# Moving the weights 16 bytes against the moving data in an FFT and feed-forward kernel

## The chip, the cores and the metric

The kernel runs on one core of one Trainium2 chip. The metric is the device time of one execution in microseconds; lower is better. The shown time of the kernel before is a median of three runs.

## The reference, cut to what matters

The reference takes the real part of a two-dimensional Fourier transform of `x` and puts every row of it through a feed-forward layer with a piecewise activation. All data are float32.

```python
batch, seq, dim = 8, 3008, 256          # x; d_ff = 2048
X = np.fft.fft(np.fft.fft(x, axis=1), axis=2).real.astype(np.float32)
h = X.reshape(-1, 256) @ w_in           # [24064, 2048]
g = np.where(h >= 1, h, np.where(h <= -1, 0.0, (h + 1) ** 2 / 4))
return (g @ w_out).astype(np.float32)   # [24064, 256]
```

The weights arrive as float64.

## The kernel before, in words

The eight batches are worked off one after the other. The transform of a batch is split into a first stage (`stage1`, seven or eight pieces), one small Nyquist product and a second stage (`stage2`, six pieces). The pieces of batch b + 1 are strewn between the matmuls of batch b. The last step of a second-stage piece is `stage2_split`: ScalarE copies the PSUM result to `pqh` (the high part, float32r) and VectorE writes the rest to `pql` (the low part, float32r).

The feed-forward part works in units. A unit is one batch, one of three chunks `k` of transform columns, and one of 16 slices `f` of d_ff; there are 8 x 3 x 16 = 384 units. Chunk 0 has 482 columns, chunks 1 and 2 have 512 (`WIDTH`). Products are made nearly float32-exact by three float32r matmuls in place of one: high weight by high data, low weight by high data, high weight by low data.

- `gemm1` (its matmuls stand on line L596) makes two PSUM tiles `uv` of a unit from three matmuls each: stationary `wh` or `wl`, moving `pqh` or `pql`. These are 6 matmuls per unit, 128 weights wide, 482 or 512 columns long.
- VectorE and ScalarE turn `uv` into the activation; `activate` and `low_halves` leave its high part in `gh` (ScalarE, L630) and its low part in `gl` (GpSimd, L647).
- `gemm2` (L684) adds the activation's product with `w_out` into four PSUM tiles `acc`: stationary `woh` or `wol`, moving `gh` or `gl`, 12 matmuls per unit. In the first 20 units, before `woh` and `wol` are made, it runs 4 native float32 matmuls on `g` and `wo` instead (`NATIVE`).

A matmul of this kernel is always two instructions on TensorE: the load of its 128 x 128 weights (PEld in the profile) and the streaming of the moving data (PE). The order of all work is written out by hand (`START`, `STEPS`, `AHEAD`, `AMID`) for the first 34 units; later it follows from the loop over units.

Where the operands lie in a partition of SBUF is set by tile sizes. `wh` and `wl` are four tiles of 8192 bytes, `woh` and `wol` tiles of 16384 bytes that take the place of raw weights loaded earlier (`raw_woh`, `raw_wol`), `pqh`, `pql`, `gh` and `gl` tiles of 4096 bytes, one row of 512 columns for each of two signs. All of these begin at multiples of 256 bytes, and a weight slice of a unit is a multiple of 512 bytes further on. `ZPAD` (40 floats ahead of the transform's `z`) and the width of `biases` (48 floats) keep what follows at such multiples. Chunk 0 alone is shifted: its 482 columns begin 28 floats, 112 bytes, into each row of its tiles (`SHIFT`). Since 28 + 512 columns would not fit in the row, the second split of chunk 0 writes only its 226 useful columns, in two parts.

Of the kernel before, what the change touches and what calls it, by code (L numbers as in the profile page):

```python
# [9 lines left out]
F32 = mybir.dt.float32  # L10
F32R = mybir.dt.float32r
U32 = mybir.dt.uint32
# [9 lines left out]
NB, S, D, FF = 8, 3008, 256, 2048  # L22
NA, NBB, NC = 64, 47, 24
P = 128
# [5 lines left out]
CH = 512  # L30
NCHUNK = 3
NFT = FF // P
ZPAD = 40
LAG = 4
SKIP = (7, 11)
EVICT_AHEAD = 150

C_ORDER = [*range(1, 8), 0, *range(8, NC)]
WIDTH = [7 * NA + 34, CH, CH]
SHIFT = [28, 0, 0]  # L40

G_ORDER = np.arange(P).reshape(XC, GPC, 2, 2).transpose(0, 3, 1, 2).reshape(-1)

# [76 lines left out]
RAW = {0: "gh", 1: "gh", 2: "woh", 3: "woh", 4: "woh", 5: "woh", 6: "wol", 7: "wol", 8: "wol", 9: "wol", 10: "rx", 11: "rx", 12: "rx", 13: "xt", 14: "pqh", 15: "pql"}  # L120
WORK = {1: "a", 2: "gl", 3: "a", 4: "h", 5: "a", 7: "a", 8: "h", 9: "gl", 11: "gl", 12: "gl", 13: "gl", 15: "gl", 14: "a"}
BUFS = {"h": 4, "a": 3, "gl": 4, "cv": 0, "rx": 3, "xt": 4}
# [3 lines left out]
LOW = {}  # L126
# [14 lines left out]
def fft_ffn_kernel(ctx: ExitStack, tc: tile.TileContext, x, xn, cst, w_in, w_out, out):  # L141
    nc = tc.nc

    wts = ctx.enter_context(tc.tile_pool(name="wts", bufs=1))
    sb = ctx.enter_context(tc.tile_pool(name="sb", bufs=1))
# [3 lines left out]
    xt, yt, zt, nyb, pq = {}, {}, {}, {}, {}  # L149
# [59 lines left out]
    cm = sb.tile([P, _OFF[6] - _OFF[2]], F32, tag="nyb", name="cm", bufs=4)  # L209
    mats = [[cm[:, (2 * m + h) * P : (2 * m + h + 1) * P] for h in range(2)] for m in range(2)]  # L210

    wh = [wts.tile([P, FF], F32R, name=f"wh{i}") for i in range(2)]
    wl = [wts.tile([P, FF], F32R, name=f"wl{i}") for i in range(2)]
    delta = wts.tile([P, NFT], F32, name="delta")
    biases = wts.tile([P, 48], F32, name="biases")
    for i, v in enumerate((0.5, -896.0 * 128, 1.0)):
        nc.vector.memset(biases[:, i : i + 1], v)
    half, below, inner = (biases[:, i : i + 1] for i in range(3))
# [4 lines left out]
    def fft_bank(b, name):  # L223

        if name in BANK:
            return ps.tile([P, CH], F32, tag=BANK[name], name=name, bufs=1)
        if b == 0 and early[0] < EARLY_BANKS:
            early[0] += 1
            return ps.tile([P, CH], F32, tag=f"acc{early[0] % 4}", name=name, bufs=1)
        return ps.tile([P, CH], F32, tag="fft", name=name, bufs=1)  # L230

    def split(hi, lo, src):
        nc.scalar.activation(hi, src, AF.Copy)
        nc.vector.tensor_tensor(lo, src, hi.bitcast(F32), op=ALU.subtract)
# [5 lines left out]
    raws, f32s, wo32, shared = {}, {}, {}, {}  # L240

    def load_w(n):
        kind, *at = jobs[n]
        if RAW[n] in ("woh", "wol"):
            if RAW[n] not in shared:
                shared[RAW[n]] = sb.tile([P, 4, CH, 2], U32, tag=RAW[n], name=f"raw_{RAW[n]}", bufs=1), iter(range(4))
            t, slots = shared[RAW[n]]
            raw = t[:, next(slots)]
        else:
            raw = sb.tile([P, CH, 2], U32, tag=RAW[n], name=f"raw_{n}", bufs=BUFS.get(RAW[n], 4))  # L250
        if kind == "in":
            src = w_in.bitcast(U32).rearrange("(h p) (o x) -> h p o x", p=P, x=2 * CH)[at[1], :, at[0] : at[0] + 1]
        else:
            m = CH // D * P
            src = w_out[at[0] * m : (at[0] + 1) * m, :].bitcast(U32).rearrange("(f p) x -> p f x", p=P)
        nc.sync.dma_start(raw.rearrange("p e two -> p (e two)").rearrange("p (f x) -> p f x", f=src.shape[1]), src)
        raws[n] = raw
# [60 lines left out]
    wo = {}  # L318

    def w_out_at(q, tag):  # L320
        if tag not in wo:
            wo[tag] = sb.tile([P, NFT, D], F32R, tag=tag, name=tag, bufs=1)
        m = CH // D
        return wo[tag][:, q * m : (q + 1) * m].rearrange("p f e -> p (f e)")

# [68 lines left out]
    s1, s2, zn = {}, {}, {}  # L394
# [7 lines left out]
    def stage1_sums(b, q):  # L402
        if q == 0:
            z = sb.tile([P, ZPAD + NC * (P + 1)], F32, tag="z", name=f"z_{b}", bufs=1)[:, ZPAD:]
            zt[b] = z[:, NC:].rearrange("p (c g) -> p c g", c=NC)
# [111 lines left out]
    def nyquist(b):  # L517
        pt = fft_bank(b, f"ny_{b}")
        nc.tensor.matmul(pt[: zn[b].shape[1], :NA], zn[b], rm[:, :NA], start=True, stop=True)  # L519
        t = sb.tile([NC, NA], F32, tag="ny", name=f"nyt_{b}", bufs=2)  # L520
        nc.scalar.activation(t, pt[:NC, :NA], AF.Copy)
        rows[b] = dr.tile([NC, NA], F32, tag="row", name=f"nyr_{b}", bufs=2)
        if b == 0:
            nc.scalar.dma_start(rows[b], t)
            return
        nc.sync.dma_start(rows[b], t)
# [20 lines left out]
        s2[b, h] = pt  # L547

    def stage2_split(b, h):
        k = h // 2  # L550
        o = (h % 2) * (CH // 2)
        end = min(o + CH // 2, WIDTH[k]) - o
        src = s2.pop((b, h)).rearrange("p i (e d) -> p i e d", e=2)
        for i, d in ((slice(0, end // NA), NA), (slice(end // NA, end // NA + 1), end % NA)):
            if d:
                at = SHIFT[k] + o + i.start * NA
                hi, lo = (t[:, :, at : at + (i.stop - i.start) * d].rearrange("p e (i d) -> p i e d", d=d) for t in pq[b, k])
                split(hi, lo, src[:, i, :, :d])

    def stage2(b, h):  # L560
        stage2_sums(b, h)
# [11 lines left out]
    units = [(0, k, f) for v in (range(FIRST), range(FIRST, NFT)) for k in range(NCHUNK) for f in v]  # L573
# [12 lines left out]
    def gemm1(i):  # L586
        b, k, f = units[i]
        n = WIDTH[k]
        at = slice(SHIFT[k], SHIFT[k] + n)
        hi, lo = (t[:, :, at] for t in pq[b, k])  # L590
        cols = slice(f * P, (f + 1) * P)
        uv = []
        for m in range(2):
            t = ps.tile([P, CH], F32, tag="uv", name=f"uv_{i}_{m}", bufs=3)
            for j, (w, r) in enumerate(((wh, hi), (wl, hi), (wh, lo))):
                nc.tensor.matmul(t[:, :n], w[m][:, cols], r[:, m], start=(j == 0), stop=(j == 2))  # L596
            uv.append(t[:, :n])
        us = sb.tile([P, CH], F32, tag="us", name=f"us_{i}", bufs=2)[:, :n]
        nc.vector.scalar_tensor_tensor(us, nyb[b, k][:, :n], delta[:, f : f + 1], uv[0], op0=ALU.mult, op1=ALU.add)  # L599
        run_steps(AHEAD.get(i, ""))  # L600
        h = sb.tile([P, 2, CH], F32, tag="h", name=f"h_{i}", bufs=4)[:, :, :n]
        nc.vector.tensor_tensor(h[:, 0], us, uv[1], op=ALU.subtract)  # L602
        last_h = nc.vector.tensor_tensor(h[:, 1], us, uv[1], op=ALU.add).ins  # L603
        a = sb.tile([P, 2, CH], F32, tag="a", name=f"a_{i}", bufs=3)[:, :, :n]

        run_steps(AMID.get(i, ""))
        for sg in signs(i):
            nc.scalar.activation(a[:, sg], h[:, sg], AF.Relu, bias=half, scale=0.5)  # L608
            nc.scalar.activation(a[:, sg], a[:, sg], AF.Square)  # L609
        fronts[i] = h, a  # L610
        after[0] = last_h.name
# [4 lines left out]
    def activate(i):  # L616
        n = WIDTH[units[i][1]]
        h, a = fronts.pop(i)
        if native(i):
            g = sb.tile([P, 2, CH], F32, tag="gh", name=f"g_{i}", bufs=4)[:, :, :n]  # L620
            acts[i] = (g,)
            nc.vector.scalar_tensor_tensor(g, a, 1.0, h, op0=ALU.min, op1=ALU.max)
            return
        at = SHIFT[units[i][1]]
        gh = sb.tile([P, 2, CH], F32R, tag="gh", name=f"gh_{i}", bufs=4)[:, :, at : at + n]
        for sg in signs(i):
            g = nc.vector.scalar_tensor_tensor(h[:, sg], a[:, sg], 1.0, h[:, sg], op0=ALU.min, op1=ALU.max).ins  # L627
            if i < n_units - 1:
                tc.add_manual_dep(g, after[0], no_sync, reason="behind the next differences")
            nc.scalar.activation(gh[:, sg], h[:, sg], AF.Copy)  # L630
        after[1] = g.name
        lows[i] = h, gh
# [3 lines left out]
    def low_halves(i):  # L636
        if i not in lows:
            return
        h, gh = lows.pop(i)
        at = SHIFT[units[i][1]]  # L640
        gl = sb.tile([P, 2, CH], F32R, tag=LOW.get(i, "gl"), name=f"gl_{i}", bufs=BUFS[LOW.get(i, "gl")])[:, :, at : at + WIDTH[units[i][1]]]
        acts[i] = gh, gl
        for sg in range(2):
            if i >= n_units - 2:
                nc.vector.tensor_tensor(gl[:, sg], h[:, sg], gh[:, sg].bitcast(F32), op=ALU.subtract)
                continue
            ins = nc.gpsimd.tensor_tensor(gl[:, sg], h[:, sg], gh[:, sg].bitcast(F32), op=ALU.subtract).ins  # L647
            if sg == 0:
                tc.add_manual_dep(ins, after[1], data_sync, reason="beside VectorE's next steps")
            else:  # L650
                tc.add_manual_dep(ins, first.name, no_sync, reason="order of issue")
            first = ins
# [139 lines left out]
    for i in range(n_units + LAG):  # L792
        if i < n_units:
            b, r = divmod(i, per)
# [27 lines left out]
        if i < n_units:  # L822
            run_steps(then)
            change = units[i][2] == (FIRST if b == 0 else 0) + LAG
            while pending and (change or units[i][2] != (FIRST if b == 0 else 0) + LAG - 1 and done < total * (r + 1 - r0) / (per - r0)):
                change = False
                w, f = pending.pop(0)
                f()
                done += w
                n = XC if b + 1 < PLAIN else XT  # L830
# [92 lines left out]
```

## Time and profile before

| | |
|---|---|
| time, median of 3 runs (lowest to highest) | 1688.47 us (1688.05 to 1688.73) |
| time of the profiled execution | 1688.27 us |
| its span, first to last instruction | 1686.4 us |
| busy share of the span: PE, PEld, DVE, ACT, POOL | 100%, 82%, 81%, 79%, 70% |
| matmul records on PE | 7722 |

Engines: PE is TensorE's matmul, PEld its weight load, DVE is VectorE, ACT ScalarE, POOL GpSimd. L684 is line 684 of the kernel. The profile's end of a matmul is modelled, and matmuls overlap in it, so that a matmul of 0.39 us does not mean a pace of 0.39 us; the pace is read from one start to the next.

### The profile page before, as it was taken

The numbers are of one execution on the slowest core, as the hardware profiler recorded it, in microseconds if no ns is written. First come the engines' busy times: TensorE is split into PE (matmuls) and PEld (weight loads), VectorE is DVE, ScalarE is ACT, GpSimd is POOL, SyncE is SP. The second block draws the span as 40 slices with busy tenths as digits, with TensorE's granted clock in tenths as the row PEclk, the third lists the DMA queues.
The fourth block names the chain that finished last, engine by engine and source line by source line (L and its number), as shares of the span: only waits on it lengthen the run. The fifth ranks groups of instructions, "written<-read, shape, count | busy, mean of one in ns | idle before, by whom it ended". The sixth has DMA issues, their size and how long they took to land.

```text
span 1686.4 us, 21438 instructions
## 1 busy us (share of the span) xinstructions
PE 1679.4 (100%) x7722; PEld 1386.4 (82%) x7722; DVE 1364.2 (81%) x1751; ACT 1328.4 (79%) x1535; POOL 1173.5 (70%) x957
## 2 busy tenths in 40 slices
PE   9999999999999999999999999999999999999999
PEld 6557888888888888888888888888888888888887
DVE  8998899877877787877887778787787777787777
ACT  5777878877788778887787878878778888777786
POOL 2447769866987568875788657886588865566664
PEclk9999999999999999999999999999999999999999
DMA  9113111100011000110010100101001000000000
GB/s 360 50 38 116 57 58 62 51 23 32 26 45 61 20 25 26 57 49 19 26 54 29 49 19 26 63 20 62 12 21 63 1 36 32 1 26 14 11 25 25
DMA packets 35705, 75.49 MB, mean 45 GB/s; under 512 B 4624, under 2 KB 13840, under 8 KB 35600
## 3 DMA queue, kind: packets, MB, share of 16 engines
q1 hardware_dynamic: 35420, 74.00, 12.4%
q8 instruction: 60, 0.98, 0.2%
q14 instruction: 45, 0.37, 0.1%
q10 hardware_dynamic: 180, 0.14, 0.0%
HBM read 46.31 MB, written 27.81 MB: 44 GB/s over the span
## 4 chain that ended last, share of the span: by engine, by line
PE 99%; DVE 0%; ACT 0%; issue 0%; POOL 0%; POOLq 0%
PE acc L684 62%; PE uv L596 31%; PE s L546 3%; PE s L415 2%; PE wps L369 1%; PE warm_bank L717 0%; ACT z L463 0%; PE s L420 0%; DVE x L167 0%; DVE z L461 0%; PE ny L519 0%; PE delta L348 0%; DVE o L702 0%; DVE wl L392 0%; ACT wh L377 0%
## 5 line engine op out<-in xcount | busy, mean ns | idle before, releaser
L647 POOL TENSOR_TENSOR gl<-h,gh 128x512 fp32r<-128x512 f32 (+1 forms) x724 | 911.0, 1279 | 399.9 <-PE acc L684 207.7
L608 ACT ACTIVATE a<-h,biases 128x1024 f32<-128x1024 f32 (+1 forms) x385 | 436.4, 1134 | 247.5 <-DVE h L603 244.7
L684 PE MATMUL acc<-gh,woh 128*128 128x512 f32 (+1 forms) x1456 | 573.2, 394 | 0.0
L684 PE MATMUL acc<-gl,woh 128*128 128x512 f32 (+1 forms) x1456 | 562.5, 386 | 0.0
L684 PE MATMUL acc<-gh,wol 128*128 128x512 f32 (+1 forms) x1456 | 560.7, 385 | 0.0
L627 DVE SCALAR_TENSOR_TENSOR h<-a,h 128x1024 f32<-128x1024 f32 (+1 forms) x365 | 490.3, 1343 | 2.0 <-ACT a L609 1.0
L599 DVE SCALAR_TENSOR_TENSOR us<-nyb,delta,uv 128x512 f32<-128x512 f32 (+1 forms) x384 | 282.7, 736 | 255.1 <-PE uv L596 254.6
L630 ACT ACTIVATE gh<-h 128x1024 fp32r<-128x1024 f32 (+1 forms) x365 | 380.0, 1041 | 52.9 <-DVE h L627 39.3
L609 ACT ACTIVATE a<-a 128x1024 f32<-128x1024 f32 (+1 forms) x385 | 395.2, 1027 | 1.1
L684 PEld LDWEIGHTS acc<-gl,woh 128*128 128x128 f32 x1456 | 273.4, 188 | 55.7
L684 PEld LDWEIGHTS acc<-gh,wol 128*128 128x128 f32 x1456 | 273.5, 188 | 49.7 <-DVE wol L331 0.3
L684 PEld LDWEIGHTS acc<-gh,woh 128*128 128x128 f32 x1456 | 273.8, 188 | 47.5
L596 PE MATMUL uv<-pqh,wh 128*128 128x512 f32 (+1 forms) x768 | 306.4, 399 | 0.6 <-ACT delta L353 0.6
L602 DVE TENSOR_TENSOR h<-us,uv 128x512 f32<-128x512 f32 (+1 forms) x384 | 260.3, 678 | 50.5 <-DVE us L599 1.0
L596 PE MATMUL uv<-pql,wh 128*128 128x512 f32 (+1 forms) x768 | 296.4, 386 | 0.0
L596 PE MATMUL uv<-pqh,wl 128*128 128x512 f32 (+1 forms) x768 | 295.6, 385 | 0.0
L603 DVE TENSOR_TENSOR h<-us,uv 128x512 f32<-128x512 f32 (+1 forms) x384 | 257.7, 671 | 0.0
L596 PEld LDWEIGHTS uv<-pqh,wl 128*128 128x128 f32 x768 | 144.1, 188 | 31.7 <-issue 5.0
L596 PEld LDWEIGHTS uv<-pqh,wh 128*128 128x128 f32 x768 | 144.3, 188 | 31.5 <-issue 3.8
L596 PEld LDWEIGHTS uv<-pql,wh 128*128 128x128 f32 x768 | 144.2, 188 | 28.8
L180 POOL TENSOR_TENSOR x<-x 120x256 f32<-120x256 f32 x84 | 85.5, 1019 | 13.9 <-DVE h L627 6.3
L449 ACT ACTIVATE z<-s 64x240 f32<-64x240 f32 (+1 forms) x196 | 69.0, 352 | 5.7 <-PE s L415 2.7
(85 smaller groups left out, 804.4 us busy)
## 6 DMA issues: line engine op xcount, KB each, us to landing
x<-in_xn_dram SPq DMA_DIRECT2D x42, 512.0 KB, 3.4
out_dram<-o SPq DMA_DIRECT2D x26, 512.0 KB, 2.7
out_dram<-o SPq DMA_DIRECT2D x14, 482.0 KB, 3.0
nyb<-nyr SPq DMA_DIRECT2D x24, 256.0 KB, 3.3
x<-in_x_dram SPq DMA_DIRECT2D x8, 512.0 KB, 7.3
raw<-in_moe_w_in_dram SPq DMA_DIRECT2D x4, 512.0 KB
raw<-in_moe_w_out_dram SPq DMA_DIRECT2D x4, 512.0 KB, 9.4
part<-o SPq DMA_DIRECT2D x4, 512.0 KB
```

The source lines that it names most:

```text
L180: return nc.gpsimd.tensor_tensor(t[:, r], t[:, r], t[:, r + 1], op=ALU.add).ins
L449: nc.scalar.activation(z[to, :, at : at + n], src[:, :, t0 : t0 + n], AF.Copy)
L596: nc.tensor.matmul(t[:, :n], w[m][:, cols], r[:, m], start=(j == 0), stop=(j == 2))
L599: nc.vector.scalar_tensor_tensor(us, nyb[b, k][:, :n], delta[:, f : f + 1], uv[0], op0=ALU.mult, op1=ALU.add)
L602: nc.vector.tensor_tensor(h[:, 0], us, uv[1], op=ALU.subtract)
L603: last_h = nc.vector.tensor_tensor(h[:, 1], us, uv[1], op=ALU.add).ins
L608: nc.scalar.activation(a[:, sg], h[:, sg], AF.Relu, bias=half, scale=0.5)
L609: nc.scalar.activation(a[:, sg], a[:, sg], AF.Square)
L627: g = nc.vector.scalar_tensor_tensor(h[:, sg], a[:, sg], 1.0, h[:, sg], op0=ALU.min, op1=ALU.max).ins
L630: nc.scalar.activation(gh[:, sg], h[:, sg], AF.Copy)
L647: ins = nc.gpsimd.tensor_tensor(gl[:, sg], h[:, sg], gh[:, sg].bitcast(F32), op=ALU.subtract).ins
L684: nc.tensor.matmul(acc[:, :n], w, g[:, sg], start=(begin and j == 0), stop=(last and j == len(terms) - 1))
```

## The change

The weights move by 16 bytes, and chunk 0's data move back to the start of their rows. `wh` and `wl` become slices of one tile `win` that begins with 4 floats of padding (`WPAD`); `woh` and `wol` are tiles with 4 floats ahead of the weights. So that the bases of the other tiles stay at multiples of 256 bytes, `biases`, `ZPAD`, the raw weight tiles and the small tile `ny` are resized. `SHIFT` goes, and with it the slices `at` in `gemm1`, `activate` and `low_halves`. The second split of chunk 0 becomes one part over all 256 columns, the last 30 of which nobody reads. What is computed in the columns that are used does not change, nor does the order of the instructions.

```diff
-ZPAD = 40
+ZPAD = 24
+WPAD = 4
-SHIFT = [28, 0, 0]
...
-    wh = [wts.tile([P, FF], F32R, name=f"wh{i}") for i in range(2)]
-    wl = [wts.tile([P, FF], F32R, name=f"wl{i}") for i in range(2)]
+    win = wts.tile([P, 4 * FF + 2 * WPAD], F32R, name="win")
+    wh, wl = ([win[:, WPAD + (2 * t + m) * FF :][:, :FF] for m in range(2)] for t in range(2))
     delta = wts.tile([P, NFT], F32, name="delta")
-    biases = wts.tile([P, 48], F32, name="biases")
+    biases = wts.tile([P, 40], F32, name="biases")
...
-                shared[RAW[n]] = sb.tile([P, 4, CH, 2], U32, tag=RAW[n], name=f"raw_{RAW[n]}", bufs=1), iter(range(4))
+                shared[RAW[n]] = sb.tile([P, 8 * CH + 4 * WPAD], U32, tag=RAW[n], name=f"raw_{RAW[n]}", bufs=1), iter(range(4))
             t, slots = shared[RAW[n]]
-            raw = t[:, next(slots)]
+            o = next(slots) * 2 * CH
+            raw = t[:, o : o + 2 * CH].rearrange("p (e two) -> p e two", two=2)
...
-            wo[tag] = sb.tile([P, NFT, D], F32R, tag=tag, name=tag, bufs=1)
+            t = sb.tile([P, NFT * D + 4 * WPAD], F32R, tag=tag, name=tag, bufs=1)
+            wo[tag] = t[:, WPAD : WPAD + NFT * D].rearrange("p (f e) -> p f e", f=NFT)
...
-        t = sb.tile([NC, NA], F32, tag="ny", name=f"nyt_{b}", bufs=2)
+        t = sb.tile([NC, NA + 20], F32, tag="ny", name=f"nyt_{b}", bufs=2)[:, :NA]
...
     def stage2_split(b, h):
-        k = h // 2
         o = (h % 2) * (CH // 2)
-        end = min(o + CH // 2, WIDTH[k]) - o
-        src = s2.pop((b, h)).rearrange("p i (e d) -> p i e d", e=2)
-        for i, d in ((slice(0, end // NA), NA), (slice(end // NA, end // NA + 1), end % NA)):
-            if d:
-                at = SHIFT[k] + o + i.start * NA
-                hi, lo = (t[:, :, at : at + (i.stop - i.start) * d].rearrange("p e (i d) -> p i e d", d=d) for t in pq[b, k])
-                split(hi, lo, src[:, i, :, :d])
+        hi, lo = (t[:, :, o : o + CH // 2].rearrange("p e (i d) -> p i e d", d=NA) for t in pq[b, h // 2])
+        split(hi, lo, s2.pop((b, h)).rearrange("p i (e d) -> p i e d", e=2))
...
-        at = slice(SHIFT[k], SHIFT[k] + n)
-        hi, lo = (t[:, :, at] for t in pq[b, k])
+        hi, lo = pq[b, k]
...
-                nc.tensor.matmul(t[:, :n], w[m][:, cols], r[:, m], start=(j == 0), stop=(j == 2))
+                nc.tensor.matmul(t[:, :n], w[m][:, cols], r[:, m, :n], start=(j == 0), stop=(j == 2))
...
-        at = SHIFT[units[i][1]]
-        gh = sb.tile([P, 2, CH], F32R, tag="gh", name=f"gh_{i}", bufs=4)[:, :, at : at + n]
+        gh = sb.tile([P, 2, CH], F32R, tag="gh", name=f"gh_{i}", bufs=4)[:, :, :n]
...
-        at = SHIFT[units[i][1]]
-        gl = sb.tile([P, 2, CH], F32R, tag=LOW.get(i, "gl"), name=f"gl_{i}", bufs=BUFS[LOW.get(i, "gl")])[:, :, at : at + WIDTH[units[i][1]]]
+        gl = sb.tile([P, 2, CH], F32R, tag=LOW.get(i, "gl"), name=f"gl_{i}", bufs=BUFS[LOW.get(i, "gl")])[:, :, : WIDTH[units[i][1]]]
```

## Rows read from the trace of the kernel before

**Rows 1.** The page: span, busy engines, granted clock by slices, chain that ended last.
```profile
span 1686.4 us, 21438 instructions
PE 1679.4 (100%) x7722; PEld 1386.4 (82%) x7722; DVE 1364.2 (81%) x1751; ACT 1328.4 (79%) x1535; POOL 1173.5 (70%) x957
...
PEclk9999999999999999999999999999999999999999
...
PE 99%; DVE 0%; ACT 0%; issue 0%; POOL 0%; POOLq 0%
```

**Rows 2.** Groups by form on PE: line, tiles, shape, count, busy us, mean ns.
```profile
L684 PE MATMUL acc<-gh,woh 128*128 128x512 f32 x992 | 392.6, 396 | 0.0
...
L596 PE MATMUL uv<-pqh,wh 128*128 128x512 f32 x512 | 202.9, 396 | 0.0
...
L684 PE MATMUL acc<-gh,woh 128*128 128x482 f32 x464 | 180.6, 389 | 0.0
...
L596 PE MATMUL uv<-pqh,wh 128*128 128x482 f32 x256 | 103.5, 404 | 0.6 <-ACT delta L353 0.6
...
L684 PE MATMUL acc<-g,wo 128*128 128x512 f32 x64 | 28.8, 592 | 0.0
```

**Rows 3.** Timeline of PE, a stretch of 512-column matmuls: start us, us, instruction.
```profile
785.63 0.39 PE L684 MATMUL acc<-gl,woh 128*128 128x512 f32 x1
...
799.91 0.39 PE L596 MATMUL uv<-pql,wh 128*128 128x512 f32 x1
```

**Rows 4.** Timeline of PE, a stretch of 482-column matmuls.
```profile
884.62 0.39 PE L684 MATMUL acc<-gh,woh 128*128 128x482 f32 x1
...
901.83 0.38 PE L596 MATMUL uv<-pqh,wl 128*128 128x482 f32 x1
```

**Rows 5.** Line L684 in a stretch of 512 columns: duration ns min/median/max.
```profile
L684 PE MATMUL acc<-gh,wol x15: 389/389/390, 784.7 to 798.3; 128*128 128x512 f32 x15
```

**Rows 6.** Line L684 in a stretch of 482 columns: duration ns min/median/max.
```profile
L684 PE MATMUL acc<-gh,woh x18: 385/385/386, 884.6 to 901.0; 128*128 128x482 f32 x18
L684 PE MATMUL acc<-gh,wol x18: 374/374/375, 884.8 to 901.2; 128*128 128x482 f32 x18
...
L684 PE MATMUL acc<-gl,woh x18: 378/378/379, 885.1 to 901.4; 128*128 128x482 f32 x18
```

**Rows 7.** Timeline of PE and PEld where a load comes late, 512 columns.
```profile
196.10 0.40 PE L684 MATMUL acc<-gl,woh 128*128 128x512 f32 x1
196.10 0.19 PEld L684 LDWEIGHTS acc<-gh,woh 128*128 128x128 f32 x1
196.34 0.39 PE L684 MATMUL acc<-gh,woh 128*128 128x512 f32 x1
...
196.59 0.41 PEld L546 LDWEIGHTS s<-cs,z 128*128 128x128 f32 x3 [0.30 <-ACT nyt L521]
```

**Rows 8.** Timeline of PE and PEld where a load comes late, 482 columns.
```profile
141.93 0.37 PE L684 MATMUL acc<-gh,wol 128*128 128x482 f32 x1
142.24 0.19 PEld L415 LDWEIGHTS s<-halves,x 120*128 120x128 f32 x1 [0.33 <-ACT z L449]
```

**Rows 9.** Timeline of PE behind a transform piece, 512 columns.
```profile
950.13 0.39 PE L684 MATMUL acc<-gh,wol 128*128 128x512 f32 x1
...
952.66 0.39 PE L596 MATMUL uv<-pqh,wh 128*128 128x512 f32 x1
```

**Rows 10.** Timeline of PE, native float32 matmuls of the first units, eight records merged.
```profile
52.82 3.59 PE L684 MATMUL acc<-g,wo 128*128 128x512 f32 x8
```

**Rows 11.** Groups by form: ScalarE's part of the split.
```profile
L233 ACT ACTIVATE pqh<-s 128x512 fp32r<-128x512 f32 x40 | 23.7, 593 | 7.1 <-PE s L546 6.5
...
L233 ACT ACTIVATE pqh<-s 128x384 fp32r<-128x384 f32 x8 | 3.9, 492 | 1.9 <-PE s L546 1.9
...
L233 ACT ACTIVATE pqh<-s 128x68 fp32r<-128x68 f32 x8 | 1.7, 210 | 0.6 <-DVE pql L234 0.6
```

## The prediction

> **What bounds the kernel now.** I read the page first: the span is 1686.4 us, PE is busy all of it, the granted clock is full (2.4 GHz) in every slice, and the chain that ended last is 99% PE [rows 1]. The other engines are busy 70 to 82%, so a faster matmul pays almost in full until the pace has fallen by several per cent, and time saved on VectorE, ScalarE or GpSimd pays nothing.
>
> Next the groups by form. `gemm1` has three groups of 512 and three of 482 columns, `gemm2` likewise; rows 2 shows one of each three, the sister groups have the same counts. So 3 x (992 + 512) = 4512 float32r matmuls have 512 columns and 3 x (464 + 256) = 2160 have 482 [rows 2]. A nanosecond on each of the long ones is 4.5 us, on each of the short ones 2.2 us. Since this change moves only addresses under these matmuls, the whole question is their pace.
>
> The pace comes from the timeline, start to start. In a stretch of 64 long matmuls it is 14.28 us / 63 = 226.7 ns [rows 3]; in 80 short ones 17.21 us / 79 = 217.8 ns [rows 4]. So 30 columns fewer save only 8.9 ns, while 30 columns at 2.4 GHz are 12.5 ns: the short ones carry about 3.6 ns that the long ones don't. The durations say where to look. The long ones are all alike, 389 to 390 ns [rows 5]. The short ones come in three kinds that stay apart through the whole stretch: 385, 374 and 378 ns, by their place among the three terms [rows 6], although shape, data tile and weight size are the same. Something other than size sets the pace of chunk 0, and chunk 0 is the one whose data lie 112 bytes into their rows.
>
> What runs beside a matmul on the same engine is the load of the next weights: it starts within 10 ns of the matmul's own start [rows 7]. In a few places it comes late, because the weights aren't ready. There a long matmul still takes 0.39 us [rows 7] and a short one 0.37 us, the lowest of its three kinds [rows 8]. These are few rows and the ends of matmuls are modelled, so it is a hint and no more: beside a load the long ones lose nothing now, the short ones 0, 4 and 11 ns, 5 on average.
>
> **The change part by part.**
>
> *Position of weights against data.* By the code, weights minus data is 0 (modulo 256 bytes) in chunks 1 and 2 and -112 in chunk 0 before; after, it is +16 in all three. No row shows a matmul at +16, so I bound it. Below: all short ones run as their fastest kind, (385 + 374 + 378) / 3 - 374 = 5.0 ns less, 2160 x 5.0 = 10.8 us gained. Behind a transform piece the long ones run unsettled for a dozen matmuls: 2.53 us / 11 = 230.0 ns in place of 226.7, 0.036 us in all [rows 9]; with 14 transform pieces in each of 7 batches that is at most 98 x 0.036 = 3.5 us. If the disturbance is the same thing, about half of it goes (many pieces fall in chunk 0, and others settle sooner): 1.8 us. Above: the long ones, which now sit at their best observed state, lose it and run like the unsettled ones, 3.3 ns x 4512 = 14.9 us. I take the lower end, since the short ones show that this position does cost time and the new one treats all chunks alike; but it is a choice between two ends that no row decides.
>
> *The second split as one part.* Per batch ScalarE's 492 + 210 ns become one of 593 ns, 109 ns less, eight times [rows 11]; VectorE's low parts go the same way. That is 0.9 us of an engine with 21% of its time free, under matmuls that never wait for it: nothing. It would be worth at most that 0.9 us if PE waited for each of these splits. The 30 extra columns are read by nobody.
>
> *Slices of `gemm1`, `activate` and `low_halves`.* Same element counts, same instructions: nothing on VectorE, ScalarE and GpSimd, unless their pace too depends on the 112 bytes; their 18 to 30% of idle time hides that.
>
> *One tile in place of four, padding, other bases.* `win` is written in pieces while other pieces are read. If the order were kept by whole tiles, the first units would wait for conversions that they don't need. It could cost only while `win` is being written, at the start. PE's idle time over the whole span is 1686.4 - 1679.4 = 7.0 us now [rows 1]; I take nothing, and as the far end that this doubles, 7.0 us. With 16 bytes of padding an odd slice of `woh` or `wol` also reaches into the next raw slot; by the written order all four raw slots of a tile have been converted before its first slice is made, so no new wait.
>
> Sum against the profiled execution's 1688.3 us, which is 1686.4 of span and 1.9 around it and lies 0.2 below the median: 1688.3 - 10.8 - 1.8 = 1675.7, and 1676 against the median.
>
> **The rivals.**
>
> *Nothing moves (1688).* Either the position of weights doesn't matter, and the three kinds in chunk 0 come from something else, or only the position modulo 128 bytes does: -112 and +16 are 128 apart, so chunk 0 would keep its pace, while the long ones settle where they are. For it: the long ones recover 226.7 ns after every disturbance, as if that state were robust. Against it: no size explains the kinds of rows 6. The Trainium skill speaks for this rival ("TensorE: Matmul & The Clock Gate", Step-by-step: what each phase is for): TensorE has one read port for the moving data and another for the weights, so that loading the next weights doesn't take read bandwidth from the running matmul. By that rule the time stays 1688; the trace agrees for the long ones [rows 5, 7] and not for the short ones [rows 6].
>
> *Slower: the long ones lose their settled state.* Position 0 may be why they sit at 226.7 ns with one single duration, while the only other position in the trace gives three kinds. If +16 gives the long ones the 5.0 ns of chunk 0, that is 4512 x 5.0 = 22.6 us; less 10.8 if chunk 0 gains, the kernel ends at 1700, and without that gain at 1711; with the unsettled 3.3 ns and no gain, at 1703. It decides from 10.8 / 4512 = 2.4 ns on: a long pace above 229.1 ns makes the kernel slower even if chunk 0 gains all.
>
> *A much larger gain.* The native float32 matmuls of the first units show what streaming alone can do: eight records of two passes over 512 columns take 3.59 us [rows 10]; one record lasts 592 ns [rows 2], so the seven steps between them are (3590 - 592) / 7 = 428 ns each, 214.1 ns a pass, and 482 columns at that rate 201.6 ns. If all that the float32r matmuls take beyond that were a clash with the loads and +16 removed it, 12.6 x 4512 + 16.2 x 2160 = 92 us would go, 1596. The Trainium skill has about the same floor (same page, Back-to-back issue gap: columns / 2.4 + 2.5 ns, 215.8 and 203.3 here), and by it the estimate would be 1608; the measured paces are 11 and 14.5 ns above it. Against it: a long matmul with no load beside it is no shorter [rows 7]. Half of it, 1642, is as far as I stretch.
>
> **How the numbers follow.** Forecast (chunk 0 freed, long ones as they are, some 1670 to 1682): 0.38. Larger gain: 0.12. Nothing moves: 0.23. Slower: 0.27. Two executions of this kernel differ by up to 0.04%, and 0.2% (3.4 us) is about what can be told from no change; the first two cases are faster by more, so faster 0.50, same 0.23, slower 0.27. Predicted 1676. The range reaches down to half of the larger gain and up to the middle of the slower cases: 1645 to 1706 leaves out about half of the larger gain and a third of the slower case, 0.15.
>
> **What would show it.** Right: in chunk 0 all three terms at 374 to 375 ns and a pace near 212 to 213 ns; 226.7 ns and 389 ns in the long stretches; PE idle 7 us of the span, as before; one 128x512 form of the split, 48 times. Wrong: three kinds of duration in the long stretches, or a pace there away from 226.7 (below 224 the larger gain, above 229.1 the slower rival), or rows 4 and 6 coming out as before.

## The result

The change makes the kernel slower: 1708.83 us (1708.57 to 1709.02, 4 runs) against 1688.40 us before (1688.05 to 1688.73, 4 runs), a ratio of 1.0121 with a 95% interval of 1.0103 to 1.0138. The forecast was a gain of 12 us; the measured time is also 2.8 us above the range. The rival that forecast a loss, "the long ones lose their settled state", gave 1700 to 1711.

The page of the changed kernel, with its span, busy engines, granted clock by slices and chain, which answer to [rows 1]:

```profile
span 1707.1 us, 21421 instructions
PE 1701.0 (100%) x7722; PEld 1391.7 (82%) x7722; DVE 1354.6 (79%) x1743; ACT 1328.7 (78%) x1527; POOL 1161.4 (68%) x957
...
PEclk9999999999999999999999999999999999999999
...
PE 99%; DVE 1%; ACT 0%; issue 0%; POOL 0%; DVEq 0%; POOLq 0%
```

PE has the same 7722 records and the same full clock, and its idle time is 1707.1 - 1701.0 = 6.1 us (7.0 before). So all of the 20.7 us of span lie in the pace of matmuls that were already there. The lines are now L591 (`gemm1`) and L677 (`gemm2`).

Two stretches of 512 columns from the timeline of PE of the changed kernel, one transform piece apart, first and last row of each (start us, us, instruction):

```profile
774.81 0.39 PE L677 MATMUL acc<-gh,wol 128*128 128x512 f32 x1
...
789.98 0.39 PE L591 MATMUL uv<-pqh,win 128*128 128x512 f32 x1
...
792.71 0.39 PE L677 MATMUL acc<-gl,woh 128*128 128x512 f32 x1
...
806.99 0.39 PE L591 MATMUL uv<-pql,win 128*128 128x512 f32 x1
```

Between the first two starts lie 65 matmuls: 15.17 us / 65 = 233.4 ns. Between the other two lie 63: 14.28 us / 63 = 226.7 ns, the pace of before [rows 3]. Same shape, same tiles, same positions of weights against data (modulo 256 bytes), and two paces. The same two stretches by line L677 (duration ns min/median/max), first the one at 233.4:

```profile
L677 PE MATMUL acc<-gh,wol x15: 394/394/394, 774.8 to 788.8; 128*128 128x512 f32 x15
L677 PE MATMUL acc<-gl,woh x15: 397/398/398, 775.0 to 789.0; 128*128 128x512 f32 x15
...
L677 PE MATMUL acc<-gh,woh x14: 394/395/396, 775.3 to 788.6; 128*128 128x512 f32 x14
L677 PEld LDWEIGHTS acc<-gh,wol x14: 192/192/192, 775.3 to 788.6; 128*128 128x128 f32 x14
...
L677 PE MATMUL acc<-gh,wol x13: 389/389/389, 793.2 to 805.4; 128*128 128x512 f32 x13
...
L677 PEld LDWEIGHTS acc<-gh,wol x13: 187/188/188, 793.6 to 805.9; 128*128 128x128 f32 x13
```

In the slower stretch the matmuls fall into kinds, as the short ones did before [rows 6], and one of the three loads is longer, 192 ns, every time. In the other stretch all is as in [rows 5]. A stretch is the run of matmuls of one width between two interruptions, mostly transform pieces. Each of the 53 long stretches of 19 or more matmuls is at one of the two paces from its first dozen matmuls to its end, and within a batch the pace mostly changes from one stretch to the next.

The short stretches are slower throughout. From the timeline again, 68 matmuls of 482 columns:

```profile
893.77 0.38 PE L677 MATMUL acc<-gl,woh 128*128 128x482 f32 x1
...
908.82 0.38 PE L677 MATMUL acc<-gh,wol 128*128 128x482 f32 x1
```

That is 15.05 us / 68 = 221.3 ns against 217.8 [rows 4]. The three kinds of [rows 6] are gone, every term now has durations from 379 to 388 ns, and the pace is worse all the same.

Averaged over all start-to-start distances below 260 ns (this leaves out only matmuls behind a transform piece or a native one), the long pace goes from 227.0 to 230.3 ns and the short one from 217.8 to 220.8: 4431 x 3.26 + 2112 x 3.02 = 14.4 + 6.4 = 20.8 us, which is the 20.7 us of the span.

The last batch has no transform pieces in it, and its 551 long matmuls show one pattern from first to last. Timeline of the changed kernel, 170 long matmuls at 39.67 us / 170 = 233.4 ns:

```profile
1600.13 0.39 PE L591 MATMUL uv<-pql,win 128*128 128x512 f32 x1
...
1639.80 0.40 PE L677 MATMUL acc<-gh,wol 128*128 128x512 f32 x1
```

The split is what the prediction said, one form 48 times (groups by form, answering to [rows 11]), and it sits on no path:

```profile
L233 ACT ACTIVATE pqh<-s 128x512 fp32r<-128x512 f32 x48 | 28.5, 595 | 10.5 <-PE s L548 10.4
```

### The profile page after: what moved, and what is told of

Its sections match the earlier page's. It is cut to its first block, busy times and chain, and to the rows that moved or that the text cites. A ratio compares the mean times of both kernels' runs of the same rounds, so it can differ in the third digit from the quotient of the medians.

```text
span 1707.1 us, 21421 instructions
## 1 busy us (share of the span) xinstructions
PE 1701.0 (100%) x7722; PEld 1391.7 (82%) x7722; DVE 1354.6 (79%) x1743; ACT 1328.7 (78%) x1527; POOL 1161.4 (68%) x957
## 4 chain that ended last, share of the span: by engine, by line
PE 99%; DVE 1%; ACT 0%; issue 0%; POOL 0%; DVEq 0%; POOLq 0%
PE acc L677 62%; PE uv L591 30%; PE s L417 2%; PE s L548 2%; PE wps L371 1%; PE warm_bank L710 0%; PE s L422 0%; ACT z L465 0%; DVE us L594 0%; DVE h L597 0%; DVE h L598 0%; PE ny L521 0%; DVE g L617 0%; DVE pql L234 0%; PE delta L350 0%
## 5 line engine op out<-in xcount | busy, mean ns | idle before, releaser
L677 PE MATMUL acc<-gh,woh 128*128 128x512 f32 (+1 forms) x1456 | 574.9, 395 | 0.0
L677 PE MATMUL acc<-gl,woh 128*128 128x512 f32 (+1 forms) x1456 | 567.1, 389 | 0.0
L677 PE MATMUL acc<-gh,wol 128*128 128x512 f32 (+1 forms) x1456 | 566.8, 389 | 0.0
L621 DVE SCALAR_TENSOR_TENSOR h<-a,h 128x1024 f32<-128x1024 f32 (+1 forms) x365 | 481.6, 1320 | 1.8 <-ACT a L604 1.0
L591 PE MATMUL uv<-pqh,win 128*128 128x512 f32 (+1 forms) x1536 | 482.1, 395 | 0.0
L591 PEld LDWEIGHTS uv<-pqh,win 128*128 128x128 f32 x1536 | 289.5, 189 | 67.6 <-issue 9.0
L677 PEld LDWEIGHTS acc<-gl,woh 128*128 128x128 f32 x1456 | 274.6, 189 | 55.8
L677 PEld LDWEIGHTS acc<-gh,wol 128*128 128x128 f32 x1456 | 275.2, 189 | 53.7 <-DVE wol L333 0.2
L677 PEld LDWEIGHTS acc<-gh,woh 128*128 128x128 f32 x1456 | 274.2, 188 | 52.7
L591 PE MATMUL uv<-pql,win 128*128 128x512 f32 (+1 forms) x768 | 298.9, 389 | 0.0
L591 PEld LDWEIGHTS uv<-pql,win 128*128 128x128 f32 x768 | 144.8, 188 | 29.8 <-DVE pql L234 0.4
L180 POOL TENSOR_TENSOR x<-x 120x256 f32<-120x256 f32 x84 | 78.9, 941 | 13.9 <-DVE h L621 6.4
L185 POOL TENSOR_TENSOR x<-x 120x256 f32<-120x256 f32 (+1 forms) x49 | 63.0, 1285 | 12.2 <-DVE h L621 5.8
L677 PE MATMUL acc<-g,wo 128*128 128x482 f32 (+1 forms) x160 | 69.7, 578 | 0.3 <-DVE g L617 0.2
```

Source lines behind the costliest of these rows:

```text
L180: return nc.gpsimd.tensor_tensor(t[:, r], t[:, r], t[:, r + 1], op=ALU.add).ins
L591: nc.tensor.matmul(t[:, :n], w[m][:, cols], r[:, m, :n], start=(j == 0), stop=(j == 2))
L677: nc.tensor.matmul(acc[:, :n], w, g[:, sg], start=(begin and j == 0), stop=(last and j == len(terms) - 1))
```

## The experiments

"Position" is where the weights begin minus where the moving data begin, modulo 256 bytes. "Long" and "short" are the mean paces of 512- and 482-column float32r matmuls, by the measure above; the text often gives the pace at which the longer stretches settle, which differs from these means. Each run stands beside the kernel before on the same chip, 1688.3 to 1688.5 us. Of e1 to e16 each was executed once, but e11 four times and e13 eleven times; executions of the kernel before lie within 1687.8 and 1688.9 us.

One thing the positions leave out: by the tile sizes, `wol` begins 256 bytes off (modulo 512) against `woh` in the kernel before and in the changed one, and no longer in e2, e3, e4, e9, e10, e12 and e16, whose `woh` and `wol` tiles are 256 bytes longer. No run moves a tile by 256 bytes alone. The changed kernel and e2 differ in these 256 bytes and lose about the same; e2, e12 and e10 agree in them and differ in position (+16, +32, +64), and their long paces are 231.1, 233.3 and 233.4 ns.

| run | long: position, ns | short: position, ns | us |
|---|---|---|---|
| before | 0, 227.0 | -112, 217.8 | 1688.4 |
| changed kernel | +16, 230.3 | +16, 220.8 | 1708.8 |
| e1 | 0, 227.2 | 0, 219.9 | 1693.0 |
| e2 | +16, 231.1 | -96, 219.1 | 1708.6 |
| e3 | +128, 232.7 | +128, 219.9 | 1717.9 |
| e4 | +16, 230.0 | 0, 219.4 | 1705.1 |
| e5 | 0, 227.0 | -112, 217.8 | 1688.6 |
| e6 (load in one place) | 0, 230.1 | -112, 217.2 | 1700.9 |
| e7 (stream in one place) | 0, 216.7 | -112, 204.4 | 1614.5 |
| e8 (484 columns) | 0, 227.4 | -112, 221.2 | 1696.7 |
| e9 | -16, 228.0 | -80, 217.1 | 1691.4 |
| e10 | +64, 233.4 | -48, 219.5 | 1720.9 |
| e11 | 0, 227.5 | -64, 222.0 | 1699.3 |
| e12 | +32, 233.3 | -32, 220.0 | 1720.7 |
| e13 | 0, 227.1 | -80, 219.0 | 1691.3 |
| e14 | +16 and 0, 227.5 | -96 and -112, 217.7 | 1690.5 |
| e15 (extra matmul) | +16, 232.3 | +16, 220.9 | 1727.0 |
| e16 | +16 and 0, 228.1 | -96 and -112, 219.2 | 1696.3 |

In every row the time follows from the two paces: 4431 times the change of the long one plus 2114 times that of the short one gives the measured difference within 1 us. Only e15 needs its added matmuls as well, which the trace records as two each: against the changed kernel 42 x 2 x 0.11 + 4431 x 2.0 = 18 us.

### Which part of the change

**e1_unshift_only**: the kernel before with `SHIFT = [0, 0, 0]` and the one-part split; weights in their old tiles.

> Only chunk 0 moves: its data go back to the start of their rows and its second split is one part; all weights stay at multiples of 256 bytes, in their old tiles. Paces before: 226.7 ns in the long stretches (512 columns), 217.8 ns in the short ones (482 columns); after: 230.3 and 220.8 on average. Theory R (what counts is the position of the weights against the data beside which they are loaded): the long ones, with a position of 0 as before, stay at 226.7; the short ones get a position that was not seen before, 0, and may go either way. Theory A (weights that stand off a multiple of 256 bytes cost by themselves): all weights stand as before, so 226.7 and 217.8, time within 2 us of 1688. Theory C (the companions: the one-part split, merged tiles, resized neighbours): the one-part split is here, so if it is the cause part of the 20 us appears, with the long ones above 226.7.

Measured 1693.02 us, +4.6. The long ones stay at 226.7, the short ones settle at 220.0: timeline of e1, 69 matmuls in 15.18 us.

```profile
886.64 0.38 PE L679 MATMUL acc<-gl,woh 128*128 128x482 f32 x1
...
901.82 0.38 PE L679 MATMUL acc<-gl,woh 128*128 128x482 f32 x1
```

The shift of 112 bytes was worth 2.1 ns a matmul on average. Theory A falls for the short ones: their weights hadn't moved. The one-part split, a part of theory C, is in this kernel and leaves the long ones alone.

**e2_weights_only**: the weights move, all else stays (`SHIFT` and two-part split included; the padding is chosen so that all other tiles stay at multiples of 256 bytes). In short:

```diff
+win = wts.tile([P, 4 * FF + 4], F32R); wh, wl = slices from win[:, 4:]
+wo[tag] = t[:, 4 : 4 + NFT * D]     # raw tiles 64 floats longer
```

> Only the weights move, 16 bytes past multiples of 256; chunk 0 keeps its shift of 112 bytes and its two-part split, and all other tiles stay at multiples of 256. Theory R: the long ones go as in the changed kernel, 230.3 on average in two kinds of stretches (226.7 and about 233), +14.5 us; the short ones get position -96 (16 - 112), not seen before. Theory A: long ones 230.3 and short ones 217.8 + 3.0 = 220.8, both as in the changed kernel, 1709 us. Theory C: if the one-part split or the resized neighbours were the cause, the time stays near 1688.

Measured 1708.61 us: the whole loss is there, without the one-part split, which this kernel does not have. That the total meets theory A's 1709 is chance: the long ones lost 4.1 ns where A had 3.3, the short ones 1.3 where A had 3.0. Timeline of e2, 168 long matmuls of the last batch in 39.20 us, 233.3 ns:

```profile
1600.66 0.40 PE L688 MATMUL acc<-gh,woh 128*128 128x512 f32 x1
...
1639.86 0.40 PE L688 MATMUL acc<-gh,woh 128*128 128x512 f32 x1
```

The merged tile and resized neighbours are in e2 too, so e2 alone does not clear them. The merged tile is in e5 below, which loses nothing; and e9, e12 and e10, with the same longer weight tiles as e2 and other positions, take 1691.4, 1720.7 and 1720.9 us, so the position decides among these.

**e4_both_16**: weights at +16 and `SHIFT = [4, 0, 0]`.

> Weights 16 bytes past multiples of 256, and chunk 0's data shifted by 16 bytes too, so that in chunk 0 the position of weights against data is 0 while both stand off the multiple; chunks 1 and 2 as in the changed kernel. Theory R: long ones 230.3 as in the changed kernel, short ones as in the run that only moves chunk 0 back (position 0 there too). Theory A: short ones 220.8 as in the changed kernel, unlike the run that only moves chunk 0 back, which has 217.8.

Measured 1705.12 us. The short ones settle at 220.0 in most stretches, as in e1 at the same position and unlike the changed kernel's 221.3.

**e5_all_32**: the kernel before with `wh`, `wl` and every tile behind them 32 bytes higher.

> As the kernel before, with every tile behind the first small constants, weights and moving data alike, 32 bytes past a multiple of 256; chunk 0 keeps its 112 bytes. Positions of weights against data are those of the kernel before: 0 and -112. Theory R (only the position against each other counts): 226.7 in every long stretch and 217.8 in the short ones, 1688 us. Theory A (being off a multiple of 256 costs): long stretches near 233 in part or all, up to 1715 us.

Measured 1688.58 us. Both patterns of before come back to the nanosecond. Timeline of e5, 70 short matmuls in 15.24 us, 217.7 ns:

```profile
885.71 0.37 PE L686 MATMUL acc<-gh,wol 128*128 128x482 f32 x1
...
900.95 0.38 PE L686 MATMUL acc<-gl,woh 128*128 128x482 f32 x1
```

So it is the position of weights against data that counts, not whether either lies at a multiple of 256. Theory R holds here, theory A is out. This is shown for one common move of 32 bytes; for 16 there is only e4 beside e1, whose short ones mostly settle alike.

### How the pace depends on the position

`SHIFT` counts floats of 4 bytes. **e3_weights_128**: as e2 with 128 bytes, no shift and the one-part split. **e9_minus_16**: weights at 240 bytes, `SHIFT` 16. **e10_plus_64**: 64 bytes, shift 28. **e12_plus_32**: 32 bytes, shift 16. **e11_shift_16**: weights at 0, shift 16.

> As the changed kernel, but the weights stand 128 bytes past multiples of 256 instead of 16, chunk 0 unshifted. If positions count only modulo 128 bytes, this is the same as weights at multiples of 256: long ones at 226.7 throughout and the short ones as in the run that only moves chunk 0 back. If they count modulo 256 bytes, both are free to differ from that run. Theory A: as the changed kernel, 230.3 and 220.8, near 1709 us.

> Weights 240 bytes past a multiple of 256, that is 16 short of one; chunk 0 shifted by 64 bytes. Positions of weights against data: -16 in chunks 1 and 2, -80 in chunk 0. By theory R the paces of this run belong to these positions. If the sign of the position does not matter (only the distance), the long stretches split like those at +16, 226.7 in about half and 233 in the rest, 230 on average; if being ahead or behind matters, they settle elsewhere, at 226.7 throughout at best.

> Weights 64 bytes past a multiple of 256, chunk 0 shifted by 112: positions +64 in chunks 1 and 2, -48 in chunk 0. If a position of 0 is a special place for 512 columns, the long stretches lie above 226.7 in part or all (230 to 234); if only the odd 16 bytes hurt and multiples of 64 are all alike, they stay at 226.7 throughout, against which the 233 ns at +128 already speaks.

> Weights 32 bytes past a multiple of 256, chunk 0 shifted by 64: positions +32 in chunks 1 and 2, -32 in chunk 0. Long stretches: if the state of 226.7 is lost by degrees with growing distance, none or few are left in it, 232 to 234 on average; if it depends on how a stretch is entered, both states are there again. Short ones: 217.8 to 221.5, as at the positions seen.

> The kernel before with chunk 0 shifted by 64 bytes instead of 112, all weights at multiples of 256: position -64 in chunk 0, 0 elsewhere. By theory R the long stretches stay at 226.7 and all difference to 1688 comes from the 2160 short matmuls, 2.16 us for each ns by which their pace leaves 217.8. Seen so far in chunk 0: 217.8 at -112, 219.0 at -96, 220.0 at 0 and +128, 221.5 at +16. If the pace changes smoothly with the position, -64 gives 219 to 221, 1691 to 1695 us; if each position has its own pattern, it can also be below 217.8, 213.3 at best (512 cycles), 1678 us, and the kernel would beat both.

The period isn't 128 bytes: at +128 no long stretch is at 226.7. At 0 all of them are where stream and loads are as in the kernel before; at +16 and -16 a third to a half, the rest at 233 and 228.5; at +32, +64 and +128 none. e11 is the miss of this group: 1699.32 us (4 runs, ratio 1.0065, 1.0048 to 1.0082), with 222.0 the worst short pace of all, between 219.5 at -48 and 217.1 at -80. There is no smooth course in the position.

Line L688 of e10 in its last batch (duration ns min/median/max):

```profile
L688 PE MATMUL acc<-gh,woh x76: 394/394/394, 1600.3 to 1678.0; 128*128 128x512 f32 x76
L688 PEld LDWEIGHTS acc<-gh,wol x76: 187/187/187, 1600.3 to 1678.0; 128*128 128x128 f32 x76
```

All three terms have 394 ns here and all loads 187, at a pace of 233.3 ns. So neither several kinds of duration nor the load of 192 ns makes the slower pace: e10 has neither, and e7 below has a load of 192 ns in every three at the fastest pace of all.

**e8_484_columns**: `WIDTH[0]` is 484.

> The kernel before with 484 instead of 482 columns in chunk 0 (two columns more that nobody reads), all positions as before. Two columns are 0.8 ns at 2.4 GHz. Theory P (a stretch settles in a repeating pattern whose length depends on where the next matmul's start falls, so that the column count matters beyond its own time): the pattern of three kinds (224, 212, 218) changes and the mean moves by more than 0.8 ns, up or down; the best that could come out is 484 x 17 / 16 cycles, 214.3 ns, the ratio at which the long ones have settled (544 cycles for 512 columns), 7 us less than before. The rival (a cost that depends on position alone): the same three kinds, 0.8 ns longer each, 218.6 ns and 1690 us.

Two columns cost 3.4 ns in place of 0.8, and the pattern of three kinds is gone. So two columns more or less change the pattern at the same position.

### What a stretch's pattern hangs on

**e15_extra_matmul**: the changed kernel with one repeated matmul in each second-stage piece of batches 1 to 7.

```diff
-        for i in range(4):
+        for i in (0, 0, 1, 2, 3) if b else range(4):
```

> The changed kernel with the first matmul of each second-stage transform piece (batches 1 to 7, 42 pieces) made twice. By itself that is 42 x 0.11 = 5 us: 1713 us if nothing else changes. In the changed kernel long stretches alternate between 226.7 and 233 ns, one piece after the other. If a stretch's state is set by the moment at which it is entered, the shares change: all or none of the stretches behind such pieces at 226.7 (down to 1702 or up to 1725 us), with one state within each stretch. If the state is a matter of buffers or batches, the same stretches are slow as before.

Measured 1727.02 us; the repeated matmuls by themselves account for 9 us of it, not the 5 expected. Of the long matmuls in stretches of 19 or more, 1802 of 3729 were at 226.7 in the changed kernel; here it is 496, and the rest run at 233. Timeline of e15, 48 matmuls in 11.20 us, 233.3 ns:

```profile
802.76 0.40 PE L591 MATMUL uv<-pqh,win 128*128 128x512 f32 x1
...
813.96 0.40 PE L677 MATMUL acc<-gh,wol 128*128 128x512 f32 x1
```

No address has changed, only the work ahead of a stretch, and stretches that were at 226.7 are now at 233. So the pattern is chosen at the entry of a stretch and held to its end; buffers and addresses alone do not choose it.

**e14_win_only_16**: only `wh` and `wl` at +16. **e16_low_weights_only**: only `wl` and `wol` at +16.

> The kernel before with the weights of the first product alone (wh, wl) 16 bytes past a multiple of 256: of the 18 long matmuls of a unit six have position +16, twelve 0. If every matmul is priced for itself by its own position, a third of the weights-only run's 18 us on the long ones appears, 6 us. If a stretch settles in one state, the twelve at 0 pull it back to 226.7 in every unit, as they do after each transform piece, and the cost is 1 to 3 us; or the six push it out each time, and it is 10 us or more.

> The kernel before with the low weights alone (wl, wol) 16 bytes past a multiple of 256. Of the three terms the second uses low weights, and during the first they are loaded. If the weights being loaded beside the stream count, the first term (high weights by high data) of the long stretches leaves 226.7 and the second and third keep it on average; if the weights in use count, the second does. 1690 to 1705 us either way.

In e14 the twelve matmuls of a unit at position 0 hold the six at +16 at 226.7 almost everywhere; the cost is 2.1 us, not a third of 18. In e16 (1696.28 us) most stretches are at 226.7 and the last batch is at 232. Over the whole run the three terms of `gemm2` are within 0.4 ns of each other, 227.8 to 228.2; in the last batch the first takes 233.1 ns to the next start, the second 232.6 and the third 231.0. All three have left 226.7 there, which neither alternative of the forecast has: whether the weights in use or those being loaded count can't be read from it.

### Whose reads they are

**e6_load_one_place**: weights with a step of zero. **e7_stream_one_place**: moving data with a step of zero. Both compute another product. The edits in `gemm1`; those in `gemm2` are alike, with the native matmuls left as they are:

```diff
# e6
-w[m][:, cols]
+w[m][:, f * P : f * P + 1].to_broadcast([P, P])
# e7
-r[:, m]
+r[:, m, :1].to_broadcast([P, n])
```

> The kernel before, but each weight load of the float32r matmuls reads one column 128 times (a step of zero) instead of 128 columns, so that the load no longer sweeps through addresses; loads and matmuls stay the same in number, order and size, and the product is another one. Theory L (the pace above columns / 2.4 GHz comes from the load's reads meeting the stream's reads in SBUF): both paces change, down towards the 214 ns (512 columns) and 202 ns (482) of the native matmuls if the meetings vanish, and the three kinds of short matmuls become one. Theory M (what is above it belongs to the float32r stream alone): 226.7 and 217.8 stay within 0.5 ns.

> The kernel before, but the moving data of the float32r matmuls are one column read 482 or 512 times (a step of zero), with the loads as before; the product is another one. Theory L: with the stream in one place the load meets it at most for a few elements of its sweep, so the pace falls to about 214 and 202 ns, or to what the loads allow. Theory M: if the stream's own reading of new addresses costs the 6%, it falls too; if the float32r matmul is that slow by itself, 226.7 and about 213 stay.

e7 falls to 1614.49 us. Its timeline, 56 long matmuls in 12.14 us, 216.8 ns:

```profile
739.76 0.38 PE L597 MATMUL uv<-pqh,wh 128*128 128x512 f32 x1
...
751.90 0.38 PE L597 MATMUL uv<-pql,wh 128*128 128x512 f32 x1
```

From the settled paces of before, 226.7 and 217.8: of the 13.4 ns by which a long matmul exceeded 512 columns at 2.4 GHz (213.3 ns), 10 vanish when the stream stays in one place; of the short ones' 17.0 ns, 13. e6 doesn't free the paces: the long ones rise to 230.1 and the short ones fall to 217.2, and again the change is one of pattern. So most of the excess needs a stream that sweeps through addresses. Whether it is the stream's own cost or its meeting with the loads isn't separated by these two runs: theory L's forecast for e6 failed, since a load in one place freed nothing on the long ones, and theory M's failed too, since the loads' addresses alone moved the long pace by 3 ns. No run keeps the stream sweeping and takes the loads away.

### The version that the positions pointed to

**e13_shift_20**: the kernel before with `SHIFT = [20, 0, 0]`.

> The kernel before with chunk 0 shifted by 80 bytes instead of 112: positions 0 in chunks 1 and 2, -80 in chunk 0, where 216.7 ns were seen with all addresses 16 bytes lower. By theory R the long stretches stay at 226.7 and the short ones settle at 216.7: 2114 x 1.0 = 2.2 us less than before, 1686.2 us. If the place in the array of addresses matters after all, the short ones go elsewhere, 217.8 to 222, 1688 to 1697 us.

Measured 1691.34 us (11 runs, ratio 1.0018, 1.0009 to 1.0027): a miss. The short ones settle at 218.4 in half of their stretches and 220.0 in the others, not at e9's 216.7. The position is the same in both, so the short pace too has more than one pattern at one position. Of the versions that compute the same product none beats the kernel before.

## Why the prediction was wrong, point by point

**What bounds the kernel.** Right. PE's pace is the whole time, the clock stayed full, and PE is 99% of the chain as before.

**Position of weights against data.** This is the step that failed, where it says "I take the lower end, since the short ones show that this position does cost time and the new one treats all chunks alike". Two things were wrong in it. First, treating all chunks alike was no reason for a gain: the long ones, at position 0, already ran at the best pace that any position gave them, as they do in e1, e5, e8, e11 and e13, which leave them there. They lost it in about half of the stretches, 14.4 us. That this is near the step's own upper bound of 14.9 is chance: the bound gave 3.3 ns to every long matmul, and the runs gave about 6.6 to half of them. Second, the short ones did not all become the kind of 374 ns: their pace of 217.8 became 220.8, +6.4 us where -10.8 was forecast. The position left behind, -112, was one of the better ones: e1 alone costs 4.6 us. The step read the spread of durations as a cost of the position, and the spread measures none: at +16 the three kinds are gone and the pace is worse, and in e10 a single duration goes with the slower long pace.

**The term of 1.8 us for unsettled long matmuls.** It was too large before any change. On average the long ones took 227.0 ns before, 0.3 to 0.4 above the settled pace, and that times 4431 is about 1.5 us for all of them; the stretch of [rows 9], with 0.036 us, opens the long ones of a batch, and most others lose 0.010 us.

**"Beside a load the long ones lose nothing now".** The few matmuls without a load beside them [rows 7, 8] were taken, as a hint, for the floor. e7 shows that the engine itself isn't held to 226.7 and to the forecast's 212 to 213: with the same loads it runs at 216.7 and 204.4 ns once the stream stays in one place. Whether a sweeping stream without loads would be faster, a few modelled ends could not tell.

**A price per matmul.** The sum multiplied nanoseconds by matmuls, as if each had a price by its own position. e14 and e15 show that a whole stretch takes one pattern; the same operands run at 226.7 or 233.4 ns by how the stretch was entered. So there is no one price for the position +16.

**The second split, the slices, one tile for four.** Right, nothing: e2 loses the same 20 us without the one-part split, e5 has the merged tile and loses nothing, and PE's idle time did not grow.

**The rivals.** The slower rival's mechanism and its deciding point (a long pace above 229.1 ns) came out. Its prices of 1700 to 1711 hold the time partly by luck: none of them has the short ones losing, which was 6.4 us, and the 22.6 us of its upper price was 14.4. Its chance of 0.27 was too low, given that the long ones were seen at 226.7 ns at position 0 alone. "Nothing moves" is out by e3 and e2: the period isn't 128 bytes, and the position counts. The Trainium skill's rule ("TensorE: Matmul & The Clock Gate", Step-by-step: what each phase is for), that loading the next weights takes no read bandwidth from the running matmul, does not cover this: moving the weights by 16 bytes cost 4.1 ns on the average long matmul in e2, and the measurement decides. The larger gain's floor is near what e7 shows, but no position that was run comes near it.

**What stays open.** Why 226.7 ns is held at position 0 and what in the entry chooses between patterns; whether the weights in use or those being loaded count (e16 doesn't tell); whether a move by 256 bytes alone would change anything; why -80 gave 216.7 in e9 and 218.4 to 220.0 in e13; and how much of the 10 ns that e7 frees would remain with no load at all, which no run shows, since in every one of them each float32r matmul brings its own load.

## What to carry to other kernels

Where matmul after matmul runs start to start on TensorE, read the pace from start to start by shape and by stretch, not from durations: a single duration for all matmuls of a shape went with the best pace here (389 ns, 226.7) and with the slower one (394 ns, 233.3 in e10). Offsets of weights against moving data are worth trying one at a time on the chip, each with its own run, and a position found good for one column count need not be good for another. Before offsetting all operands for the sake of one chunk, price what the other chunks can lose first: here they had twice as many matmuls.

## What the runs showed that was not expected

Moving the weights by 16 bytes against the data moved the time by 20 us, moving both by 32 bytes together moved it by 0.3 us (e2, e5). With identical operands a stretch of 512-column float32r matmuls has two paces, 226.7 and 233.4 ns, held for up to 551 matmuls in a row, and in the changed kernel the pace mostly flips from one stretch to the next, behind a transform piece. In its slower pattern one load in three takes 192 ns in place of 187 to 188, but e10 is as slow with all loads at 187. A float32r matmul whose moving operand has a step of zero runs at 216.7 ns for 512 columns and 204.4 for 482, 4.5 and 6.1% less than the same matmul over distinct columns.
